# P times V with V as the moving operand in two column tiles, and the result picked and weighted by VectorE, in a one-core decode kernel

## The chip, the cores and the metric

The kernel runs on one core of one Trainium2 chip. The metric is the device time of one execution in microseconds (us). Times quoted are medians of repeated runs. Executions over 1.5% slower than the fastest of the same kernel are left out of the means. A ratio is the mean time of one kernel's runs over the mean of the other's runs of the same rounds, so it is not quite the ratio of the medians quoted; its interval is a 95% one. The span in a profile, from the first to the last instruction, is about 2 us shorter than the time.

## The reference

One decode step, 8 batch rows, sequence length 1: layer norm, attention of 32 query heads on 8 KV heads over the last 2048 of 8192 cached positions, output projection, then a small MLP block. What matters here:

```python
q = (layernorm(x) @ wq)                              # 8 rows, 32 heads of 128
k = k_cache[:, :, Sk - W:, :]                        # W = 2048, 8 KV heads of 128
v = v_cache[:, :, Sk - W:, :]                        # each KV head serves 4 query heads
p = softmax(einsum("bhqd,bhkd->bhqk", q, k) * 128**-0.5)
o = einsum("bhqk,bhkd->bhqd", p, v)
h = x + o.reshape(B, 1, 4096) @ wo
...                                                  # MLP: w3 (512x1792), gelu, w4 (1792x512)
```

K, V and the weights are 79.2 MB, all read once.

## The kernel before

Work is cut into tiles of 2 MB: four KV heads of one batch row, 128 partitions by 64 chunks of 128 columns. Each batch row has two K tiles and two V tiles, each handled in four quarters (`NT`, index `qi`); a quarter is one step of the main loop. Ten buffers hold tiles, and they are filled in the order of use by one queue.

Per step, TensorE transposes 16 chunks of K into PSUM (`pe_T`), ScalarE copies one half out (`act_Elo`), VectorE the other (`dve_Ehi`), and two steps later TensorE multiplies them with q (`pe_QK`). When a batch row's scores are complete, the row maximum (`dve_max`, VectorE) and two exp (`act_exp`, ScalarE) follow, then TensorE transposes P, VectorE masks it (`dve_pT`), and P times V runs.

```python
        def pe_PV(e, v):                      # v = 2 * b + gq: one V tile
            # [...] waits for the tile; the order of (qi, cc), 64 pairs, differs for the last tile
            ot = misc[:, OT].rearrange("d (g a r) -> d g a r", g=GL, r=R)[:, :, gq, :]
            pt = pT_sb[:, :, :].rearrange("p c (g x) -> p c g x", g=GL)
            for n, (qi, cc) in enumerate(seq):
                c = qi * CC + cc
                # [...] waits for the two halves of pT, and of the last V tile
                o = R * (NT * gq + qi)
                ins = e.matmul(ot, slots[:, slot, c * DH:(c + 1) * DH], pt[:, cc, :, o:o + R],
                               start=(n == 0), stop=(n == C - 1), skip_group_check=True)
            ins.then_inc(sem_PV, 1)

        def dve_combine(e, b):                # once per batch row: times 1/L, into oT_all
            e.wait_ge(sem_PV, 2 * (b + 1))
            e.wait_ge(sem_rL, b + 1)
            e.tensor_tensor(oT_all[:, :, b].rearrange("p (q g r) -> p g q r", g=GL, r=R),
                            misc[:, OT].rearrange("p (g q r) -> p g q r", g=GL, r=R),
                            rL[:, :].rearrange("p (g q r) -> p g q r", g=GL, r=R), ALU.mult).then_inc(sem_oT, 1)

        for p in range(NITEM + 2 * NT):       # one step = one quarter of a K tile
            b, t = divmod(p - 2 * NT, 2 * NT) # t = 0..7 within the softmax and PV of batch row b
            if p < NITEM:                     # transposes and evictions of K, one batch row ahead
                # [...] PE: pe_T(k, p); ACT: act_Elo(p); DVE: dve_Ehi(p)
            # [...] PE: pe_QK(p - 2), at t == 0 also pe_QK(p - 1)
            if t == 0:
                DV.append(lambda e, b=b: dve_max(e, b))
            if t in (1, 2):
                AC.append(lambda e, b=b, h=t - 1: act_exp(e, b, h))
            if t == TP:                       # TP = 3
                # [...] PE: transposes of P; DVE: sums of P, dve_pT in two halves; PE, DVE: 1/L
                PE.append(lambda e, b=b: pe_PV(e, 2 * b))
            elif t == 7:
                PE.append(lambda e, b=b: pe_PV(e, 2 * b + 1))
                DV.append(lambda e, b=b: dve_combine(e, b))
```

V is the stationary operand: 64 weight loads of 128x128, and 64 matmuls of 16 columns, per V tile. Each engine works through its list in order, so the place of a piece in the list decides what it can delay (measured: in the changed kernel the row maximum starts at 75.39 us, behind the sums listed ahead of it, though its scores are complete at about 74.3). After the last batch row come the output projection (128 matmuls of 8 columns with Wo stationary) and the MLP.

Of the kernel before, what the change touches and what calls it, by code (L numbers as in the profile page):

```python
# [6 lines left out]
dt = mybir.dt  # L7
# [6 lines left out]
H = 32  # L14
DH = 128
# [22 lines left out]
def bass_sequential_preLN__sliding_block_cached__mixer_s_mlp__decode_kernel(  # L38
# [24 lines left out]
    with es:  # L63
# [28 lines left out]
        pT_sb = sb([128, CC, 128], dt.bfloat16, "pT_sb")  # L92
        maskT = sb([128, 128], dt.bfloat16, "maskT")
        sel = sb([128, H], dt.float32, "sel")
# [4 lines left out]
        lsel = sb([128, H], dt.float32, "lsel")  # L99
        rL = sb([128, H], dt.float32, "rL")  # L100
        iota_f = sb([128, 128], dt.float32, "iota_f")
        ones_f = sb([128, 128], dt.float32, "ones_f")
# [27 lines left out]
        LB = slice(256, 256 + H)  # L130
        misc = ps_t([128, 512], dt.float32, "misc")
        OT = slice(256, 256 + H)
# [27 lines left out]
        sem_PV = S("sem_PV")  # L160
        sem_oT = S("sem_oT")
# [32 lines left out]
        def pool_prog(e):  # L194
# [3 lines left out]
            e.memset(scratch[:], 1.0)  # L198
            e.memset(ones_f[:], 0.25).then_inc(sem_pool, 1)
# [92 lines left out]
        def dve_ident(e):  # L292
# [4 lines left out]
            with nc.allow_low_precision("sums of one 1 and zeros"):  # L297
                ins = e.tensor_reduce(sel[:, 0:GL], ident_f[:, :].rearrange("p (a g) -> p g a", g=GL), AX.X, ALU.add)
            chain(e, ins, "dve_self", dve_self)
            ins = e.tensor_copy(maskT[:, :].rearrange("p (g x) -> p g x", g=GL),  # L300
                                bass.AP(tensor=sel[:, :].tensor, offset=0, ap=[[H, 128], [1, GL], [0, 128 // GL]]))
            chain(e, ins, "dve_self", dve_self)
            e.tensor_reduce(sel[:, :].rearrange("p (a r) -> p a r", r=R),
                            ident_f[:, :].rearrange("p (a q r) -> p a r q", q=NT, r=R),
                            AX.X, ALU.add).then_inc(sem_dveP, 1)
# [170 lines left out]
        def dve_lsel(e, b):  # L476
            e.wait_ge(sem_exp, 2 * (b + 1))
            if b >= 1:
                e.wait_ge(sem_LB, b)
            j = b % 2  # L480
            ins = e.tensor_tensor(lsum[:, :], lcol[:, j, 0:1], lcol[:, j, 1:2], ALU.add)  # L481
            chain(e, ins, "dve_self", dve_self)
            e.tensor_scalar(lsel[:, :], sel[:, :], lsum[:, :], None, ALU.mult).then_inc(sem_lsel, 1)

        def pe_LB(e, b):
            e.wait_ge(sem_lsel, b + 1)
            if b >= 1:
                e.wait_ge(sem_rL, b)
            e.matmul(b6[:, LB], ones_f[:, :], lsel[:, :], start=True, stop=True).then_inc(sem_LB, 1)

        def dve_rL(e, b):
            e.wait_ge(sem_LB, b + 1)
            if b >= 1:
                e.wait_ge(sem_oT, b)
            e.reciprocal(rL[:, :], b6[:, LB]).then_inc(sem_rL, 1)

        def dve_pT(e, b, half):
            e.wait_ge(sem_PT, 2 * b + half + 1)
            if b >= 1:
# [3 lines left out]
            mask_rep = bass.AP(tensor=maskT[:, :].tensor, offset=0, ap=[[128, 128], [0, hc], [1, 128]])  # L503
            e.tensor_tensor(pT_sb[:, half * hc:(half + 1) * hc, :],  # L504
                            kT_ps[n % 2][:, half * W // 2:(half + 1) * W // 2].rearrange("p (c x) -> p c x", x=128),
                            mask_rep, ALU.mult).then_inc(sem_pT, 1)

        def pe_PV(e, v):
# [5 lines left out]
            if gq == 0 and b >= 1:  # L514
                e.wait_ge(sem_oT, b)
            ot = misc[:, OT].rearrange("d (g a r) -> d g a r", g=GL, r=R)[:, :, gq, :]
            pt = pT_sb[:, :, :].rearrange("p c (g x) -> p c g x", g=GL)
            if last:
                seq = [(qi, cc) for qi in range(NT) for cc in range(CC)]
            else:  # L520
                seq = [(qi, cc) for lo in (0, CC // 2) for qi in range(NT) for cc in range(lo, lo + CC // 2)]
            ins = None
            for n, (qi, cc) in enumerate(seq):
                c = qi * CC + cc
                if gq == 0 and n in (0, C // 2):
                    e.wait_ge(sem_pT, 2 * b + 1 + (n > 0))
                if last and c in V_CUT:
                    e.wait_ge(sem_vlast[V_CUT.index(c)], 16)
                o = R * (NT * gq + qi)
# [229 lines left out]
```

## Time and profile before

198.81 us, median of 3 runs (198.02 to 198.83).

| | before |
|---|---|
| bytes read | 79.2 MB, at about 428 GB/s in mid-stream |
| one batch row | 19.3 to 19.6 us of stream (from K tile to K tile, 69.91 to 147.66 us), about 17.8 us of TensorE work |
| last V half landed, last PV done | 178.66 us, 180.1 us |
| output projection | from 180.57 to 186.8 us |

The page's slice rows. The span is cut into 40 equal slices; a digit is the busy share in tenths, PEclk the granted TensorE clock in tenths:

```profile
span 196.6 us, 6327 instructions
...
PEclk9999999999996999999999699969999979755557
DMA  6999999999999999999999999999999999999990
GB/s 215 427 410 430 427 430 427 430 430 430 430 422 427 430 425 430 427 430 430 427 427 433 430 430 427 428 423 423 427 430 433 430 388 382 425 405 338 398 358 21
...
```

The DMA engines are full from the second slice to the last but one: the stream is the limit. The clock is at a half in the tail (0.50 from 178 to 186.5 us).

The groups of instructions by shape, of the kernel before: line, engine, operation, output and inputs, shape, count, then busy us and the mean ns of one, then idle time before them:

```profile
...
L530 PE MATMUL misc<-pT_sb,slots 128*128 128x16 bf16 x1024 | 28.6, 170 | 3.7 <-DVE pT_sb L504 1.9 <-DMA slots<-in_A_v_cache_dram 1.6 <-issue 0.2
L530 PEld LDWEIGHTS misc<-pT_sb,slots 128*128 128x128 bf16 x1024 | 27.3, 97 | 7.7 <-issue 5.9 <-DMA slots<-in_A_v_cache_dram 1.8
...
L693 PE MATMUL b<-slots,gT 128*8 128x256 bf16 x28 | 2.8, 382 | 0.0
...
L537 DVE TENSOR_TENSOR oT_all<-misc,rL 128x32 bf16<-128x32 f32 x8 | 2.4, 300 | 16.0 <-PE misc L530 16.0
...
```

A narrow matmul lasts 170 ns, but 1024 of them take 28.6 us: one starts every 28 ns. The last matmuls of the MLP (L693) run in two column tiles.

The table of two stretches, each one batch row: bounds and length in us, busy us of PE, PEld, DVE, ACT and POOL with counts, then granted clock, DMA share, GB/s:

```profile
...
69.91:89.17 19.26, 17.05 (x313) 12.38 (x310) 9.28 (x20) 10.27 (x12) 0.00 (x0) 1.00 1.01 427
89.17:108.64 19.47, 17.07 (x306) 12.38 (x306) 8.98 (x19) 10.27 (x12) 0.00 (x0) 1.00 1.01 428
...
```

TensorE is busy for 17.06 of some 19.4 us while the DMA share is 1: it has time to spare. The waits of TensorE in total us, times and longest:

```profile
...
PE kT_ps L406 <- DMA slots<-in_A_k_cache_dram: 7.9, 6, 1.7
...
PE S_ps L603 <- issue: 1.9, 1, 1.9
...
```

It waited for K tiles six times (one of them the first). From the first row, 19.26 us less one wait of 1.51 us inside it, TensorE's own need of about 17.8 us per batch row follows. The stream's own pace shows where TensorE waits for it: the K tiles of 89.17 and 147.66 us, three batch rows apart, both ended such a wait, so a batch row of stream takes 19.5 us.

The timeline of TensorE in the tail (start, us, engine, line, operation, count, idle before and what ended it):

```profile
...
158.88 1.15 PE L406 MATMUL kT_ps<-ident_b,slots 128*128 128x128 bf16 x16 [1.25 <-DMA slots<-in_A_k_cache_dram]
...
174.16 1.88 PE L530 MATMUL misc<-pT_sb,slots 128*128 128x16 bf16 x64
...
178.66 0.97 PE L530 MATMUL misc<-pT_sb,slots 128*128 128x16 bf16 x30 [1.41 <-DMA slots<-in_A_v_cache_dram]
...
180.74 3.15 PE L603 MATMUL S_ps<-oT_all,slots 128*128 128x8 bf16 x112
184.12 0.40 PE L603 MATMUL S_ps<-oT_all,slots 128*128 128x8 bf16 x9 [0.23 <-DMA slots<-in_A_wo_dram]
186.46 0.33 PE L603 MATMUL S_ps<-oT_all,slots 128*128 128x8 bf16 x7 [1.93 <-issue]
```

The transposes of the last K tile begin at 158.88 us, as soon as it has landed. PV of the last tile but one takes 1.88 us at a granted clock of 0.50, little more than the 1.75 us it takes at 1.00 (78.12 us). Inside the projection TensorE stands for 1.93 us with nothing to wait for ("issue"), after the 121st matmul.

### The profile page before, as it was taken

How to read it: one execution, taken by the hardware profiler on the slowest of the kernel's cores; microseconds unless marked ns; L12 is line 12 of the kernel's file. 1: busy time of each engine (PE TensorE's matmuls, PEld its weight loads, DVE VectorE, ACT ScalarE, POOL GpSimd, SP SyncE). 2: the span in 40 equal slices, each digit the busy share in tenths (PEclk: the TensorE clock that was granted, in tenths of full speed). 3: DMA queues.
4: the chain of work that ended last, by engine and by line, in shares of the span. 5: the costliest groups of instructions: out<-in, count | busy, mean ns of one | idle time of the engine just before them, and what ended most of it. 6: DMA issues, size and time to landing. Idle time of an engine off the chain costs nothing.

```text
span 196.6 us, 6327 instructions
## 1 busy us (share of the span) xinstructions
PE 159.2 (81%) x2808; PEld 118.4 (60%) x2808; DVE 82.4 (42%) x184; ACT 90.6 (46%) x109; POOL 4.7 (2%) x15
## 2 busy tenths in 40 slices
PE   2027999789999998988897889899979879395555
PEld 0027865566768675755675667677756656185553
DVE  7501445543463457335623473356336514330040
ACT  3300565945392648434753384457535635240040
POOL 8000000000000000000000000000000000000000
PEclk9999999999996999999999699969999979755557
DMA  6999999999999999999999999999999999999990
GB/s 215 427 410 430 427 430 427 430 430 430 430 422 427 430 425 430 427 430 430 427 427 433 430 430 427 428 423 423 427 430 433 430 388 382 425 405 338 398 358 21
DMA packets 10569, 79.57 MB, mean 405 GB/s; under 512 B 672, under 2 KB 4784, under 8 KB 6192
## 3 DMA queue, kind: packets, MB, share of 16 engines
q1 hardware_dynamic: 10544, 79.19, 96.5%
q8 instruction: 22, 0.36, 0.7%
q14 instruction: 3, 0.02, 0.0%
HBM read 79.18 MB, written 0.01 MB: 403 GB/s over the span
## 4 chain that ended last, share of the span: by engine, by line
DMA 56%; PE 28%; SPq 6%; issue 4%; DVE 3%; ACT 3%; ACTq 0%; DVEq 0%
DMA slots<-in_A_k_cache_dram 51%; PE kT_ps L406 16%; PE S_ps L438 6%; SPq L266 5%; DMA slots<-in_A_wo_dram 5%; PE misc L530 3%; ACT P_sb L472 1%; PE b L693 1%; ACT kT_sb L417 1%; PE misc L663 1%; DVE pT_sb L504 1%; PE S_ps L603 0%; PE S_ps L621 0%; DVE mtile L450 0%; SPq L258 0%
## 5 line engine op out<-in xcount | busy, mean ns | idle before, releaser
L417 ACT ACTIVATE kT_sb<-kT_ps 128x1024 bf16<-128x1024 bf16 x64 | 65.5, 1023 | 75.6 <-PE kT_ps L406 75.6
L406 PEld LDWEIGHTS kT_ps<-ident_b,slots 128*128 128x128 bf16 x1024 | 63.7, 104 | 30.0 <-issue 21.5
L406 PE MATMUL kT_ps<-ident_b,slots 128*128 128x128 bf16 x1024 | 73.2, 231 | 7.9 <-DMA slots<-in_A_k_cache_dram 7.9
L423 DVE COPY kT_sb<-kT_ps 128x1024 bf16<-128x1024 bf16 x64 | 43.4, 687 | 61.4 <-PE kT_ps L406 61.4
L438 PE MATMUL S_ps<-kT_sb,qstrip 128*32 128x512 bf16 x256 | 39.0, 614 | 0.0
L530 PEld LDWEIGHTS misc<-pT_sb,slots 128*128 128x128 bf16 x1024 | 27.3, 97 | 7.7 <-issue 5.9
L530 PE MATMUL misc<-pT_sb,slots 128*128 128x16 bf16 x1024 | 28.6, 170 | 3.7 <-DVE pT_sb L504 1.9
L472 ACT ACTIVATE P_sb<-S_ps,mtile 128x1024 bf16<-128x1024 f32 x16 | 17.8, 1113 | 4.8 <-DVE mtile L461 4.4
L406 PE MATMUL kT_ps<-ident_b,P_sb 128*128 128x128 bf16 x128 | 10.6, 231 | 6.6 <-ACT P_sb L472 5.5
L406 PEld LDWEIGHTS kT_ps<-ident_b,P_sb 128*128 128x128 bf16 x128 | 7.8, 103 | 12.0 <-issue 4.4
L504 DVE TENSOR_TENSOR pT_sb<-kT_ps,maskT 128x1024 bf16<-128x1024 bf16 x16 | 10.4, 684 | 0.1
L438 PEld LDWEIGHTS S_ps<-kT_sb,qstrip 128*32 128x32 bf16 x256 | 6.0, 94 | 6.5 <-issue 1.2
L537 DVE TENSOR_TENSOR oT_all<-misc,rL 128x32 bf16<-128x32 f32 x8 | 2.4, 300 | 16.0 <-PE misc L530 16.0
L585 ACT ACTIVATE std<-var,eps_t 128x8 f32<-128x8 f32 x1 | 0.3, 301 | 14.3 <-DVE var L636 14.3
L450 DVE TENSOR_REDUCE mtile<-S_ps 128x1 f32<-128x512 f32 x8 | 5.5, 692 | 3.1 <-PE S_ps L438 3.1
L361 PE MATMUL S_ps<-xlnT,slots 128*128 128x8 bf16 x128 | 3.6, 168 | 3.6 <-DMA slots<-in_A_wq_dram 3.6
L361 PEld LDWEIGHTS S_ps<-xlnT,slots 128*128 128x128 bf16 x128 | 3.5, 104 | 3.6 <-issue 3.6
L603 PE MATMUL S_ps<-oT_all,slots 128*128 128x8 bf16 x128 | 3.9, 168 | 2.2 <-issue 1.9
L341 PE MATMUL b<-ident_b,xln_b 8*128 8x8 bf16 x4 | 0.3, 175 | 6.4 <-DVE xln_b L318 6.4
L603 PEld LDWEIGHTS S_ps<-oT_all,slots 128*128 128x128 bf16 x128 | 3.6, 104 | 2.3 <-issue 2.0
L481 DVE TENSOR_TENSOR lsum<-lcol 128x1 f32<-128x1 f32 x8 | 1.3, 158 | 8.0 <-ACT P_sb L472 8.0
L341 PEld LDWEIGHTS b<-ident_b,xln_b 8*128 8x128 bf16 x4 | 0.2, 116 | 7.3 <-DVE xln_b L318 7.3
(75 smaller groups left out, 59.8 us busy)
## 6 DMA issues: line engine op xcount, KB each, us to landing
slots<-in_A_k_cache_dram SPq DMA_DIRECT2D x16, 2048.0 KB, 41.5
slots<-in_A_v_cache_dram SPq DMA_DIRECT2D x15, 2048.0 KB, 43.3
slots<-in_A_wq_dram SPq DMA_DIRECT2D x1, 4096.0 KB, 12.2
slots<-in_A_wo_dram SPq DMA_DIRECT2D x1, 2048.0 KB, 43.8
slots<-in_A_v_cache_dram SPq DMA_DIRECT2D x2, 1024.0 KB, 13.6
slots<-in_B_w_dram SPq DMA_DIRECT2D x1, 1792.0 KB, 11.6
slots<-in_A_wo_dram SPq DMA_DIRECT2D x1, 1024.0 KB, 16.5
slots<-in_A_wo_dram SPq DMA_DIRECT2D x2, 512.0 KB, 13.0
```

Of the source, the lines that this page charges most:

```text
L266: e.dma_start(dst[:, f0:f0 + (h1 - h0) * D].rearrange("p (h n) -> p h n", n=D), A_wo[h0 * 128:h1 * 128, :].rearrange("(h p) n -> p h n", p ...
L361: ins = e.matmul(S_ps[:, 0, h * B:(h + 1) * B], wq_v[:, kc, h * DH:(h + 1) * DH], xlnT[:, kc * B:(kc + 1) * B], start=(kc == 0), stop=(kc ...
L406: ins = e.matmul(kT_ps[n % 2][:, c * 128:(c + 1) * 128], src[:, c * 128:(c + 1) * 128], ident_b[:, :], is_transpose=True)
L417: e.activation(kT_sb[:, i % NKT, 0:W // 2], kT_ps[step_of[("k", i)] % 2][:, 0:W // 2], ACT.Copy).then_inc(sem_Elo, 1)
L423: e.tensor_copy(kT_sb[:, i % NKT, W // 2:W], kT_ps[step_of[("k", i)] % 2][:, W // 2:W]).then_inc(sem_Ehi, 1)
L438: ins = e.matmul(S_ps[32 * gl:32 * (gl + 1), b % 2, :], qstrip[:, b, GL * gq + gl, o:o + 32], kv[:, gl, :, :], start=(gq == 0 and qi == 0) ...
L450: ins = e.tensor_reduce(mtile[:, 2, 0:1], S_ps[:, j, :], AX.X, ALU.max)
L472: e.activation(P_sb[:, half * W // 2:(half + 1) * W // 2].rearrange("r (k g) -> r k g", g=GL), s_rep, ACT.Exp, bias=mtile[:, j, 0:1], scal ...
L504: e.tensor_tensor(pT_sb[:, half * hc:(half + 1) * hc, :], kT_ps[n % 2][:, half * W // 2:(half + 1) * W // 2].rearrange("p (c x) -> p c x", ...
L530: ins = e.matmul(ot, slots[:, slot, c * DH:(c + 1) * DH], pt[:, cc, :, o:o + R], start=(n == 0), stop=(n == C - 1), skip_group_check=True)
L537: e.tensor_tensor(oT_all[:, :, b].rearrange("p (q g r) -> p g q r", g=GL, r=R), misc[:, OT].rearrange("p (g q r) -> p g q r", g=GL, r=R), ...
L603: ins = e.matmul(hT_ps[:, k * B:(k + 1) * B], wo_at(h)[:, k * 128:(k + 1) * 128], oT_all[:, h, :], start=False, stop=(h == H - 1), skip_gr ...
```

## The change

The intent: exchange the operands of P times V. P (64 columns: four heads by four quarters by four rows) becomes stationary, and V moves, 512 columns at a time, in two column tiles of the array, so that a V tile needs 16 matmuls in place of 64. The result is a matrix of 64 rows by four quarters, of which only the blocks with matching quarter are wanted. VectorE picks and normalises them: four dependent operations multiply each quarter's block with a mask that holds 1/L and add them up; one fp32 matmul per V tile then sums the two column tiles and transposes, and VectorE copies the result.

The diff, cut to its core (constants, the set-up of the selection masks, the new layout of the P mask, one more small operation in the 1/L step and some waits are left out):

```diff
@@ pe_PV @@
-            for n, (qi, cc) in enumerate(seq):
-                [...]
-                ins = e.matmul(ot, slots[:, slot, c * DH:(c + 1) * DH], pt[:, cc, :, o:o + R],
-                               start=(n == 0), stop=(n == C - 1), skip_group_check=True)
+            if v >= 1:
+                e.wait_ge(sem_O1, v)
+            vq = slots[:, slot, :].rearrange("p (q c d) -> p c q d", q=NT, d=DH)
+            groups = [(0, 2), (2, 4)] if last else [(0, NT)]
+            for n, (q0, q1) in enumerate(groups):
+                if last:
+                    e.wait_ge(sem_vlast[n], 16)
+                for cc in range(CC):
+                    [...]
+                    a = cc % 2
+                    ins = e.matmul(misc[64 * a:64 * (a + 1), q0 * DH:q1 * DH].rearrange("p (q d) -> p q d", d=DH),
+                                   pT_sb[:, gq, cc, :], vq[:, cc, q0:q1, :],
+                                   start=(n == 0 and cc < 2), stop=(n == len(groups) - 1 and cc >= CC - 2),
+                                   tile_position=(0, 64 * a), skip_group_check=True)
             ins.then_inc(sem_PV, 1)

-        def dve_combine(e, b): [...]
+        def dve_O1(e, v):
+            [...]
+            ins = e.tensor_scalar(o_sum[:, :], misc[:, 0:DH], mrl[:, gq, 0:1], None, ALU.mult)
+            for q in range(1, NT):
+                chain(e, ins, "dve_self", dve_self)
+                ins = e.scalar_tensor_tensor(o_sum[:, :], misc[:, q * DH:(q + 1) * DH], mrl[:, gq, q:q + 1],
+                                             o_sum[:, :], ALU.mult, ALU.add)
+            ins.then_inc(sem_O1, 1)
+
+        def pe_oT(e, v):
+            e.wait_ge(sem_O1, v + 1)
+            [...]
+            e.matmul(b6[:, OT], o_sum[:, :], hsel[:, :], start=True, stop=True).then_inc(sem_oTm, 1)
+
+        def dve_oT(e, v):
+            [...]
+            e.tensor_copy(oT_all[:, GL * R * gq:GL * R * (gq + 1), b], b6[:, OT]).then_inc(sem_oT, 1)
@@ main loop, behind the transposes and evictions of a step @@
+            for v, (at_o1, at_mm, at_cp) in late.items():
+                if p == at_o1:
+                    DV.append(lambda e, v=v: dve_O1(e, v))
+                if p == at_mm:
+                    PE.append(lambda e, v=v: pe_oT(e, v))
+                if p == at_cp:
+                    DV.append(lambda e, v=v: dve_oT(e, v))
@@ t == TP @@
                 PE.append(lambda e, b=b: pe_PV(e, 2 * b))
+                late[2 * b] = (p + 1, p + 2, p + 3)
             elif t == 7:
                 PE.append(lambda e, b=b: pe_PV(e, 2 * b + 1))
-                DV.append(lambda e, b=b: dve_combine(e, b))
+                late[2 * b + 1] = (p + 1, p + 2, p + 3)
@@ behind the loop @@
+        DV.append(lambda e: dve_O1(e, NTILE - 1))
+        PE.append(lambda e: pe_oT(e, NTILE - 1))
+        DV.append(lambda e: dve_oT(e, NTILE - 1))
```

So the sums of a V tile come one step after its PV, the summing matmul two steps after, the copy three.

More of the change, by code (lines that the diff above doesn't have):

```diff
@@ L91, in bass_sequential_preLN__sliding_block_cached__mixer_s_mlp__decode_kernel @@
         P_sb = sb([128, CC * 128], dt.bfloat16, "P_sb")
-        pT_sb = sb([128, CC, 128], dt.bfloat16, "pT_sb")
-        maskT = sb([128, 128], dt.bfloat16, "maskT")
-        sel = sb([128, H], dt.float32, "sel")
+        pT_sb = sb([128, 2, CC, 64], dt.bfloat16, "pT_sb")
+        maskT = sb([128, CC // 2 * GL, 32], dt.bfloat16, "maskT")
+        sel = sb([128, GL], dt.float32, "sel")
+        headc = sb([128, NT * R], dt.float32, "headc")
+        lspread = sb([128, 128], dt.float32, "lspread")
+        par_sel = sb([128, 2, GL * R], dt.float32, "par_sel")
+        hsel = sb([128, GL * R], dt.float32, "hsel")
+        gq_of = sb([128, 2], dt.float32, "gq_of")
+        qi_of = sb([128, NT], dt.float32, "qi_of")
+        mrl = sb([128, 2, NT], dt.float32, "mrl")
+        o_sum = sb([128, DH], dt.float32, "o_sum")
         mtile = sb([128, 3, 32], dt.float32, "mtile")
@@ L98, in bass_sequential_preLN__sliding_block_cached__mixer_s_mlp__decode_kernel @@
         lsum = sb([128, 1], dt.float32, "lsum")
-        lsel = sb([128, H], dt.float32, "lsel")
-        rL = sb([128, H], dt.float32, "rL")
+        lsel = sb([128, 2], dt.float32, "lsel")
+        rL = sb([128, 2], dt.float32, "rL")
         iota_f = sb([128, 128], dt.float32, "iota_f")
-        ones_f = sb([128, 128], dt.float32, "ones_f")
         oT_all = sb([128, H, B], dt.bfloat16, "oT_all")
@@ L129, in bass_sequential_preLN__sliding_block_cached__mixer_s_mlp__decode_kernel @@
         xT_ps = b6[:, 0:256].bitcast(dt.bfloat16)
-        LB = slice(256, 256 + H)
+        LB = slice(256, 258)
+        OT = slice(320, 320 + GL * R)
         misc = ps_t([128, 512], dt.float32, "misc")
-        OT = slice(256, 256 + H)
         H3 = slice(384, 384 + FC * B)
@@ L160, in bass_sequential_preLN__sliding_block_cached__mixer_s_mlp__decode_kernel @@
         sem_PV = S("sem_PV")
+        sem_O1 = S("sem_O1")
+        sem_oTm = S("sem_oTm")
         sem_oT = S("sem_oT")
@@ L197, in pool_prog @@
             e.memset(zrow_b[:], 0.0)
-            e.memset(scratch[:], 1.0)
-            e.memset(ones_f[:], 0.25).then_inc(sem_pool, 1)
+            e.memset(scratch[:], 1.0).then_inc(sem_pool, 1)
             e.iota(iota_f[:], [[1, 128]], base=0, channel_multiplier=-1,
@@ L299, in dve_ident @@
             chain(e, ins, "dve_self", dve_self)
-            ins = e.tensor_copy(maskT[:, :].rearrange("p (g x) -> p g x", g=GL),
-                                bass.AP(tensor=sel[:, :].tensor, offset=0, ap=[[H, 128], [1, GL], [0, 128 // GL]]))
+            ins = e.tensor_copy(maskT[:, :, :].rearrange("p (c g) x -> p c g x", g=GL),
+                                bass.AP(tensor=sel[:, :].tensor, offset=0, ap=[[GL, 128], [0, CC // 2], [1, GL], [0, 32]]))
             chain(e, ins, "dve_self", dve_self)
-            e.tensor_reduce(sel[:, :].rearrange("p (a r) -> p a r", r=R),
-                            ident_f[:, :].rearrange("p (a q r) -> p a r q", q=NT, r=R),
-                            AX.X, ALU.add).then_inc(sem_dveP, 1)
+            with nc.allow_low_precision("sums of one 1 and zeros"):
+                e.tensor_reduce(headc[:, :].rearrange("p (g r) -> p g r", r=R),
+                                ident_f[:, :].rearrange("p (g x r) -> p g r x", g=GL, r=R), AX.X, ALU.add)
+                e.tensor_reduce(par_sel[:, :, :].rearrange("p a (g r) -> p a g r", r=R),
+                                ident_f[:, :].rearrange("p (a g q r) -> p a g r q", a=2, g=GL, r=R), AX.X, ALU.add)
+                e.tensor_reduce(gq_of[:, :], ident_f[:, :].rearrange("p (g a x) -> p a g x", g=GL, a=2), AX.XY, ALU.add)
+                ins = e.tensor_reduce(qi_of[:, :], ident_f[:, :].rearrange("p (a q r) -> p q a r", q=NT, r=R), AX.XY, ALU.add)
+            chain(e, ins, "dve_self", dve_self)
+            hc = bass.AP(tensor=headc[:, :].tensor, offset=0, ap=[[NT * R, 128], [R, GL], [0, NT], [1, R]])
+            for a in range(2):
+                e.tensor_scalar(lspread[:, 64 * a:64 * (a + 1)].rearrange("p (g q r) -> p g q r", g=GL, r=R),
+                                hc, 0.25, None, ALU.mult)
+            e.tensor_tensor(hsel[:, :], par_sel[:, 0, :], par_sel[:, 1, :], ALU.add).then_inc(sem_dveP, 1)
         DV.append(dve_ident)
@@ L482, in dve_lsel @@
             chain(e, ins, "dve_self", dve_self)
-            e.tensor_scalar(lsel[:, :], sel[:, :], lsum[:, :], None, ALU.mult).then_inc(sem_lsel, 1)
+            e.tensor_scalar(lsel[:, :], gq_of[:, :], lsum[:, :], None, ALU.mult).then_inc(sem_lsel, 1)
         def pe_LB(e, b):
@@ L487, in pe_LB @@
             if b >= 1:
+                e.wait_ge(sem_oT, 2 * b)
                 e.wait_ge(sem_rL, b)
-            e.matmul(b6[:, LB], ones_f[:, :], lsel[:, :], start=True, stop=True).then_inc(sem_LB, 1)
+            e.matmul(b6[:, LB], lspread[:, :], lsel[:, :], start=True, stop=True).then_inc(sem_LB, 1)
         def dve_rL(e, b):
             e.wait_ge(sem_LB, b + 1)
-            if b >= 1:
-                e.wait_ge(sem_oT, b)
-            e.reciprocal(rL[:, :], b6[:, LB]).then_inc(sem_rL, 1)
+            ins = e.reciprocal(rL[:, :], b6[:, LB])
+            chain(e, ins, "dve_self", dve_self)
+            e.tensor_tensor(mrl[:, :, :],
+                            bass.AP(tensor=rL[:, :].tensor, offset=0, ap=[[2, 128], [1, 2], [0, NT]]),
+                            bass.AP(tensor=qi_of[:, :].tensor, offset=0, ap=[[NT, 128], [0, 2], [1, NT]]),
+                            ALU.mult).then_inc(sem_rL, 1)
         def dve_pT(e, b, half):
@@ L502, in dve_pT @@
             hc = CC // 2
-            mask_rep = bass.AP(tensor=maskT[:, :].tensor, offset=0, ap=[[128, 128], [0, hc], [1, 128]])
-            e.tensor_tensor(pT_sb[:, half * hc:(half + 1) * hc, :],
-                            kT_ps[n % 2][:, half * W // 2:(half + 1) * W // 2].rearrange("p (c x) -> p c x", x=128),
-                            mask_rep, ALU.mult).then_inc(sem_pT, 1)
+            e.tensor_tensor(pT_sb[:, :, half * hc:(half + 1) * hc, :].rearrange("p a c (g x) -> p (c g) a x", g=GL),
+                            kT_ps[n % 2][:, half * W // 2:(half + 1) * W // 2].rearrange("p (m a x) -> p m a x", a=2, x=16),
+                            maskT[:, :, :].rearrange("p m (a x) -> p m a x", a=2), ALU.mult).then_inc(sem_pT, 1)
         def pe_PV(e, v):
@@ L513, in pe_PV @@
                 e.wait_ge(sem_slot[slot], 16 * use)
-            if gq == 0 and b >= 1:
-                e.wait_ge(sem_oT, b)
-            ot = misc[:, OT].rearrange("d (g a r) -> d g a r", g=GL, r=R)[:, :, gq, :]
-            pt = pT_sb[:, :, :].rearrange("p c (g x) -> p c g x", g=GL)
-            if last:
-                seq = [(qi, cc) for qi in range(NT) for cc in range(CC)]
-            else:
-                seq = [(qi, cc) for lo in (0, CC // 2) for qi in range(NT) for cc in range(lo, lo + CC // 2)]
@@ L522, in pe_PV @@
-            ins = None
-            for n, (qi, cc) in enumerate(seq):
-                c = qi * CC + cc
-                if gq == 0 and n in (0, C // 2):
-                    e.wait_ge(sem_pT, 2 * b + 1 + (n > 0))
-                if last and c in V_CUT:
-                    e.wait_ge(sem_vlast[V_CUT.index(c)], 16)
-                o = R * (NT * gq + qi)
-                ins = e.matmul(ot, slots[:, slot, c * DH:(c + 1) * DH], pt[:, cc, :, o:o + R],
-                               start=(n == 0), stop=(n == C - 1), skip_group_check=True)
@@ L532, in pe_PV @@
-            ins.then_inc(sem_PV, 1)
-        def dve_combine(e, b):
-            e.wait_ge(sem_PV, 2 * (b + 1))
-            e.wait_ge(sem_rL, b + 1)
-            e.tensor_tensor(oT_all[:, :, b].rearrange("p (q g r) -> p g q r", g=GL, r=R),
-                            misc[:, OT].rearrange("p (g q r) -> p g q r", g=GL, r=R),
-                            rL[:, :].rearrange("p (g q r) -> p g q r", g=GL, r=R), ALU.mult).then_inc(sem_oT, 1)
+            if v >= 1:
+                e.wait_ge(sem_O1, v)
@@ new lines, in pe_PV @@
+            vq = slots[:, slot, :].rearrange("p (q c d) -> p c q d", q=NT, d=DH)
+            groups = [(0, 2), (2, 4)] if last else [(0, NT)]
+            ins = None
+            for n, (q0, q1) in enumerate(groups):
+                if last:
+                    e.wait_ge(sem_vlast[n], 16)
+                for cc in range(CC):
+                    if gq == 0 and cc in (0, CC // 2):
+                        e.wait_ge(sem_pT, 2 * b + 1 + (cc > 0))
+                    a = cc % 2
[3 more added lines that the diff above has]
+                                   tile_position=(0, 64 * a), skip_group_check=True)
@@ new lines, in pe_PV @@
+            ins.then_inc(sem_PV, 1)
+        def dve_O1(e, v):
+            b, gq = divmod(v, 2)
+            e.wait_ge(sem_PV, v + 1)
+            if gq == 0:
+                e.wait_ge(sem_rL, b + 1)
+            if v >= 1:
+                e.wait_ge(sem_oTm, v)
+            ins = e.tensor_scalar(o_sum[:, :], misc[:, 0:DH], mrl[:, gq, 0:1], None, ALU.mult)
+            for q in range(1, NT):
+                chain(e, ins, "dve_self", dve_self)
+                ins = e.scalar_tensor_tensor(o_sum[:, :], misc[:, q * DH:(q + 1) * DH], mrl[:, gq, q:q + 1],
+                                             o_sum[:, :], ALU.mult, ALU.add)
+            ins.then_inc(sem_O1, 1)
@@ L541, in bass_sequential_preLN__sliding_block_cached__mixer_s_mlp__decode_kernel @@
+        def pe_oT(e, v):
+            e.wait_ge(sem_O1, v + 1)
+            e.wait_ge(sem_rL, v // 2 + 1)
+            if v >= 1:
+                e.wait_ge(sem_oT, v)
+            e.matmul(b6[:, OT], o_sum[:, :], hsel[:, :], start=True, stop=True).then_inc(sem_oTm, 1)
+        def dve_oT(e, v):
+            b, gq = divmod(v, 2)
+            e.wait_ge(sem_oTm, v + 1)
+            e.tensor_copy(oT_all[:, GL * R * gq:GL * R * (gq + 1), b], b6[:, OT]).then_inc(sem_oT, 1)
+        late = {}
         for p in range(NITEM + 2 * NT):
@@ L593, in pe_proj @@
             e.wait_ge(sem_exp, 2 * NB)
-            e.wait_ge(sem_oT, NB)
+            e.wait_ge(sem_oT, 2 * NB)
             for k in range(KC):
```

## The prediction

> **What bounds it now.** The input stream. The slice rows show the DMA engines at 90% or more from the second slice to the last but one, at about 428 GB/s; 79.2 MB at that rate is 185 us. In the table of stretches one pair of batch halves (two K and two V tiles) takes 19.3 to 19.9 us, DMA share 1.00. TensorE needs about 17.8 us of it: the waits view has it idle for K tiles five times, 1.1 to 1.7 us each, in mid-stream. V is reissued far ahead (issue to landing 41 to 43 us), so a late slot release starves nothing. After the last V half lands (178.66 in the timeline) a serial tail follows: last PV to 180.1, combine, 128 output-projection matmuls (third Wo piece at 184.1, then 1.93 us of "issue" idle), 186.8, then the MLP, 9.8 us.
>
> **What changes.** PV: 64 matmuls of 16 columns per V tile, 1.75 us (about 27 ns each), become 16 of 512 columns in two column tiles. Transposes stream 128 columns in 62 ns (16 in 1.00 us), so 512 should cost about 0.22 to 0.25 us, an estimate. That two column tiles run together the MLP's last matmuls show: 28 of 256 columns in 2.64 us, while one of them lasts 382 ns. So 8 pairs cost 1.8 to 2.0 us: no gain, although busy instructions fall by 750. [...]
>
> Added per V tile: on VectorE four dependent 128x128 operations from PSUM, about 0.3 us each (the 128x32 one takes 0.30, the 128x512 reduction 0.69), so 1.25 us, and a 0.3 us copy instead of half a 0.30 us combine; on TensorE an fp32 128x16 matmul, 0.3 us (the 128x32 one is 0.3 to 0.4). The mask multiply should stay at 0.68 us, and the extra 1/L step is small.
>
> **What is on the path.** Mid-stream almost nothing directly. But the second V tile's four operations come ahead of the row maximum in VectorE's order, and the end of the scores matmuls and of those PV matmuls lie only about 2 us apart: I expect maximum, exp and P transposes to move about 1 us per batch. With the summing matmuls TensorE's need rises from 17.8 to some 19.2 to 20.3 us, about the stream's 19.6. So it stops catching up: the backlog of about 2 us that it has at batch 0 (first K waits only at 89 us) stays, or grows by some us.
>
> In the tail two new chains (1.25 weighted sum + 0.4 matmul + 0.35 copy) stand in series, the first before the last PV, and PV's 512-column streams feel the half clock of the last slices (0.5), which 16-column matmuls did not. The Wo wait and the 1.93 us stall hide part. Sum: +1 to +4 us; a grown backlog could add more.
>
> **Time.** 201.0 us; 8 in 10 between 197.8 and 206. Faster by over 2%: 0.04; within: 0.70; slower: 0.26.
>
> **Right or wrong, in the profile.** PV per tile at 1.8 to 2.0 us mid-stream; VectorE busy from 82 to about 105 us; DMA still full to about 190 us; fewer K waits by TensorE, and later; row maximum about 1 us later after the scores; projection starting at 182 to 186 instead of 180.6; matmuls from 2808 to about 2090.
>
> **What would make it wrong.** Column tiles that run serially, or weight loads that show (PV near 3.5 us): TensorE then bounds every batch, 208 us or more. Full backlog recovery, or the instruction stall vanishing with the shorter program: 198 us. A mask multiply slowed by its 16-element runs delays every batch.

One sentence, on weight loads, is cut from the recorded text at the mark: no trace of this case shows what it said. The sum of +1 to +4 us held no term for it and stands as it was.

## The result, and the profile after

205.37 us (median of 4 runs, 203.53 to 205.77) against 198.74 us (4 runs): ratio 1.0321, interval 1.0276 to 1.0366. The change is 3.2% slower.

The page's slice rows of the changed kernel:

```profile
span 203.4 us, 4997 instructions
...
PEclk9999999999999999999999999999999999859757
DMA  6999999999999999999999999999999999999300
GB/s 208 419 435 432 425 438 419 432 428 420 435 432 422 441 420 435 422 428 438 419 435 424 435 428 425 432 432 428 419 441 422 386 432 408 395 390 411 134 0 5
...
```

The stream's last full slice is the 37th, and the last two slices and more, some 13 us, move next to nothing; before the change that stretch was one slice of 5 us. The stream no longer sets the end. The granted clock is no worse than before (0.958 in the mean against 0.905).

The groups of the changed kernel that are new:

```profile
...
L547 PE MATMUL misc<-slots,pT_sb 128*64 128x512 bf16 x240 | 30.5, 398 | 2.1 <-DVE pT_sb L525 2.1
...
L563 DVE SCALAR_TENSOR_TENSOR o_sum<-misc,mrl,o_sum 128x128 f32<-128x128 f32 x48 | 16.8, 351 | 1.7
L547 PEld LDWEIGHTS misc<-slots,pT_sb 128*64 128x64 bf16 x272 | 15.7, 113 | 14.7 <-issue 7.1
...
L572 PE MATMUL b<-hsel,o_sum 128*128 128x16 f32 x32 | 6.3, 273 | 9.5 <-DVE o_sum L563 9.5
...
```

A wide matmul lasts 398 ns, but two run at once: in the PV of 81.47 us the two of a pair start 4 to 31 ns apart, and the 8 pairs take 1.86 us, 0.23 us each, at a granted clock of 1.00. The table of two stretches, each one batch row from TensorE's point of view:

```profile
...
83.33:103.50 20.17, 18.21 (x217) 11.49 (x216) 11.35 (x29) 10.27 (x12) 0.00 (x0) 1.00 1.00 428
143.80:163.92 20.12, 18.17 (x216) 11.44 (x215) 11.35 (x29) 10.28 (x12) 0.00 (x0) 1.00 1.01 416
...
```

A batch row takes 20.15 us, the same every time (P's transposes start at 59.14, 79.28, 99.43, 119.58, 139.73 and 159.88 us). That is 0.65 us more than the 19.5 us that the stream needed before. The waits of TensorE:

```profile
...
PE b L572 <- DVE o_sum L563: 9.5, 16, 1.6
...
PE kT_ps L424 <- DVE kT_sb L441: 2.2, 6, 0.4
...
PE kT_ps L424 <- DMA slots<-in_A_k_cache_dram: 1.2, 1, 1.2
...
```

In place of six waits for K tiles there is one (the first of all), and there are 16 for the weighted sums. Where these lie shows the timeline of TensorE within one batch row:

```profile
...
75.53 0.40 PE L572 MATMUL b<-hsel,o_sum 128*128 128x16 f32 x2 [0.20 <-DVE o_sum L563]
...
77.75 1.05 PE L424 MATMUL kT_ps<-ident_b,slots 128*128 128x128 bf16 x16 [0.37 <-DVE kT_sb L441]
...
81.47 1.92 PE L547 MATMUL misc<-slots,pT_sb 128*64 128x512 bf16 x16 [0.30 <-DVE pT_sb L525]
...
84.87 1.07 PE L424 MATMUL kT_ps<-ident_b,slots 128*128 128x128 bf16 x16
86.60 0.40 PE L572 MATMUL b<-hsel,o_sum 128*128 128x16 f32 x2 [0.66 <-DVE o_sum L563]
...
```

The summing matmul of the first V tile (start 86.60) stands in TensorE's list right behind the transposes of 84.87, but VectorE's sums, which begin only behind an eviction of K, are not done: 0.66 us idle. For the second V tile (75.53) the wait is 0.20 us. The transposes at 77.75 wait another 0.37 us for an eviction of K by VectorE. VectorE's timeline shows why that one is late:

```profile
...
73.37 0.69 DVE L441 COPY kT_sb<-kT_ps 128x1024 bf16<-128x1024 bf16 x1 [2.70 <-PE kT_ps L424]
73.98 0.34 DVE L560 TENSOR_SCALAR o_sum<-misc,mrl 128x128 f32<-128x128 f32 x1
74.36 1.12 DVE L563 SCALAR_TENSOR_TENSOR o_sum<-misc,mrl,o_sum 128x128 f32<-128x128 f32 x3
75.39 0.68 DVE L468 TENSOR_REDUCE mtile<-S_ps 128x1 f32<-128x512 f32 x1
...
```

The four operations of the sums (73.98 to 75.48) come ahead of the row maximum (75.39), which could have started when the scores were complete, at about 74.3. So the maximum, the evictions behind it and exp are about 1 us late.

The tail of the changed kernel:

```profile
...
163.92 1.07 PE L424 MATMUL kT_ps<-ident_b,slots 128*128 128x128 bf16 x16
...
179.86 3.62 PE L547 MATMUL misc<-slots,pT_sb 128*64 128x512 bf16 x16
185.09 0.40 PE L572 MATMUL b<-hsel,o_sum 128*128 128x16 f32 x2 [1.61 <-DVE o_sum L563]
185.41 1.94 PE L547 MATMUL misc<-slots,pT_sb 128*64 128x256 bf16 x32
...
189.93 3.53 PE L654 MATMUL S_ps<-oT_all,slots 128*128 128x8 bf16 x128
...
```

The transposes of the last K tile begin at 163.92 us, against 158.88 us before: TensorE comes out of mid-stream 5.04 us late; this is the lag of the texts below. PV of the last tile but one takes 3.62 us at a granted clock of 0.50, against 1.92 us at 1.00 in mid-stream. The projection starts at 189.8 us, 9.2 us later than before, but its 128 matmuls run without a stop, and it ends at 193.5 us, 6.7 us later than before.

### The profile page after: what moved, and what is told of

It reads as the page before. It is cut to its first block, busy times and chain, and to the rows that moved or that the text cites. A ratio compares the mean times of both kernels' runs of the same rounds, so it can differ in the third digit from the quotient of the medians.

```text
span 203.4 us, 4997 instructions
## 1 busy us (share of the span) xinstructions
PE 164.8 (81%) x2088; PEld 107.8 (53%) x2088; DVE 103.2 (51%) x270; ACT 90.9 (45%) x109; POOL 4.6 (2%) x14
## 4 chain that ended last, share of the span: by engine, by line
PE 50%; DVE 20%; issue 13%; DMA 8%; ACT 7%; SPq 0%; ACTq 0%; DVEq 0%
PE kT_ps L424 20%; PE misc L547 16%; DMA slots<-in_A_k_cache_dram 8%; PE S_ps L456 8%; DVE o_sum L563 8%; ACT P_sb L490 5%; DVE o_sum L560 3%; DVE mtile L468 2%; DVE pT_sb L525 2%; PE b L572 2%; PE S_ps L654 2%; ACT kT_sb L435 1%; PE b L744 1%; PE misc L714 1%; DVE mrow L470 1%
## 5 line engine op out<-in xcount | busy, mean ns | idle before, releaser
L424 PEld LDWEIGHTS kT_ps<-ident_b,slots 128*128 128x128 bf16 x1024 | 60.3, 101 | 30.5 <-issue 29.2
L424 PE MATMUL kT_ps<-ident_b,slots 128*128 128x128 bf16 x1024 | 70.0, 224 | 3.4 <-DVE kT_sb L441 2.2
L456 PE MATMUL S_ps<-kT_sb,qstrip 128*32 128x512 bf16 x256 | 38.3, 613 | 0.0
L547 PE MATMUL misc<-slots,pT_sb 128*64 128x512 bf16 (+1 forms) x272 | 32.4, 383 | 2.1 <-DVE pT_sb L525 2.1
L547 PEld LDWEIGHTS misc<-slots,pT_sb 128*64 128x64 bf16 x272 | 15.7, 113 | 14.7 <-issue 7.1
L490 ACT ACTIVATE P_sb<-S_ps,mtile 128x1024 bf16<-128x1024 f32 x16 | 17.8, 1115 | 11.6 <-DVE mtile L479 11.5
L563 DVE SCALAR_TENSOR_TENSOR o_sum<-misc,mrl,o_sum 128x128 f32<-128x128 f32 x48 | 16.8, 351 | 1.7
L572 PE MATMUL b<-hsel,o_sum 128*128 128x16 f32 x32 | 6.3, 273 | 9.5 <-DVE o_sum L563 9.5
L572 PEld LDWEIGHTS b<-hsel,o_sum 128*128 128x128 f32 x32 | 4.8, 188 | 13.9 <-DVE o_sum L563 13.9
L560 DVE TENSOR_SCALAR o_sum<-misc,mrl 128x128 f32<-128x128 f32 x16 | 5.5, 344 | 6.3 <-PE misc L547 6.3
```

The lines of the kernel that those rows point to most:

```text
L424: ins = e.matmul(kT_ps[n % 2][:, c * 128:(c + 1) * 128], src[:, c * 128:(c + 1) * 128], ident_b[:, :], is_transpose=True)
L456: ins = e.matmul(S_ps[32 * gl:32 * (gl + 1), b % 2, :], qstrip[:, b, GL * gq + gl, o:o + 32], kv[:, gl, :, :], start=(gq == 0 and qi == 0) ...
L490: e.activation(P_sb[:, half * W // 2:(half + 1) * W // 2].rearrange("r (k g) -> r k g", g=GL), s_rep, ACT.Exp, bias=mtile[:, j, 0:1], scal ...
L547: ins = e.matmul(misc[64 * a:64 * (a + 1), q0 * DH:q1 * DH].rearrange("p (q d) -> p q d", d=DH), pT_sb[:, gq, cc, :], vq[:, cc, q0:q1, :], ...
L560: ins = e.tensor_scalar(o_sum[:, :], misc[:, 0:DH], mrl[:, gq, 0:1], None, ALU.mult)
L563: ins = e.scalar_tensor_tensor(o_sum[:, :], misc[:, q * DH:(q + 1) * DH], mrl[:, gq, q:q + 1], o_sum[:, :], ALU.mult, ALU.add)
```

## The experiments

My theory after this: nothing in the new form is too slow in itself. TensorE waits for the sums in its list, and the maximum waits behind the sums in VectorE's list. That lifts a batch row from about 17.8 to 20.15 us, just over what the stream needs, and only the excess is paid, gathered row by row (six rows lie between the transposes of 43.03 us and the last K tile at 163.92 us). The rivals: the added VectorE work and the wide PV cost the time wherever they stand; or the loss is made in the tail.

### First: the summing matmul of the first V tile one step later

```diff
-                late[2 * b] = (p + 1, p + 2, p + 3)
+                late[2 * b] = (p + 1, p + 3, p + 4)
```

> Only the summing matmul of the first V tile of each batch, and its copy, move one step later in program order; all work is kept. In the changed kernel TensorE stands 0.65 us before that matmul in every batch, waiting for VectorE's weighted sums. Order theory (the loss in mid-stream is TensorE waiting in program order for the sums, twice per batch, which made a batch 20.15 us against some 19.6 us of stream): that wait goes to about 0, a batch takes about 19.5 us, the lag of about 5 us at the last K tile shrinks to about 0.5 to 1.5 us, time about 201 (200 to 202). Rival (the added VectorE work and the new PV form as such cost the time, wherever they stand): a batch stays at about 20.1 us and the time at about 205.

Measured: 200.28 us (198.49 to 200.45), ratio to before 1.0063 (1.0016 to 1.011). P's transposes start every 19.28 us. The waits of TensorE:

```profile
...
PE b L572 <- DVE o_sum L563: 4.9, 9, 1.6
...
PE kT_ps L424 <- DMA slots<-in_A_k_cache_dram: 1.2, 1, 1.2
...
```

The waits for the sums fall from 16 to 9 and from 9.5 to 4.9 us: seven waits of 0.65 us are gone, one per batch row. 0.87 us less per batch row brought back 5 us of 6.6. The same work is done, so the rival of work as such falls. The profile is of the fastest of the four runs (198.49 us), and in it the lag is gone (the last K tile begins at 158.25 us); where the other three, 200.23 to 200.45 us, lose about 1.8 us no trace shows.

### Second: the sums of the second V tile behind the row maximum

```diff
+                if kind == "p" and i >= 1 and c == CT // 2:    # between the halves of P's transposes
+                    pe_oT(e, 2 * i - 1)
 [...]
+                if b >= 1:                                      # ahead of the sums of P
+                    DV.append(lambda e, b=b: dve_oT(e, 2 * b - 1))
 [...]
-                late[2 * b + 1] = (p + 1, p + 2, p + 3)
+                late[2 * b + 1] = (p + 3, None, None)
```

> Only the weighted sums of the second V tile of each batch move: behind the row maximum of the next batch instead of ahead of it, their summing matmul between the two halves of the P transposes, where TensorE waits for exp anyway. All work is kept. Order theory: row maximum, exp and P transposes come about 1 us earlier, the stalls before the transposes that follow go, a batch needs about 18.9 us of TensorE, so the stream bounds again (19.6 us) and the lag at the last K tile goes to about 0 to 1 us; time about 200.5 (199.5 to 202). Rival (work as such): unchanged, about 205.

Measured: 198.18 us (198.07 to 198.25), ratio to before 0.9977 (0.9957 to 0.9997). P's transposes start every 19.15 us (57.45 to 134.05), 1.0 us less, and the last K tile begins at 157.46 us. The wait of 0.65 us of the first V tiles is still there:

```profile
...
PE b L574 <- DVE o_sum L565: 7.8, 9, 1.6
...
```

I expected 200.5 us, with a tail that costs 2 us; the whole loss was gone instead. That was a hint that the wide tail costs less than I thought.

### Third: both moves

The two diffs above together.

> Both moves together, all work kept. Order theory: TensorE needs about 18.2 us per batch, waits for K tiles again as before the change (several waits), the mid-stream loss is gone, and what is left against the kernel before is the tail alone: PV in wide streams at the half clock (3.6 against 1.9 us for the last tile but one) and two chains of weighted sums, summing matmul and copy. Time 200 to 201.5, hardly better than the better of the two single moves. Rival (work as such): about 205.

Measured: 198.13 us (197.72 to 199.77), ratio to before 0.9991 (0.9944 to 1.0037), better than the 200 to 201.5 us that I expected with the wide tail. While TensorE had no K tile to wait for, P's transposes were 18.29 us apart (56.62 to 74.91). Then it waits for K tiles again, as the kernel before did:

```profile
...
PE kT_ps L426 <- DMA slots<-in_A_k_cache_dram: 6.4, 5, 2.4
...
```

Here the batch row has 1.9 us less than in the changed kernel, twice the saving of a single move, and the time is no better than with the second move alone (198.13 against 198.18 us). Below the stream's pace nothing more was won.

### Fourth: the old PV in the last batch row only

The changed kernel, mid-stream untouched; PV and normalisation of the last batch row as before the change:

```diff
+            if b == NB - 1:
+                [...] for n, (qi, cc) in enumerate(seq):      # as before: V stationary, 16 columns
+                    pt = pT_sb[:, gq, cc, :].rearrange("p (g x) -> p g x", g=GL)[:, :, R * qi:R * (qi + 1)]
+                    ins = e.matmul(ot, slots[:, slot, c * DH:(c + 1) * DH], pt, [...])
 [...]
-        DV.append(lambda e: dve_O1(e, NTILE - 1))
-        PE.append(lambda e: pe_oT(e, NTILE - 1))
-        DV.append(lambda e: dve_oT(e, NTILE - 1))
+        DV.append(lambda e: dve_combine(e, NB - 1))           # with 1/L of this batch row in the old form
```

> The changed kernel with PV and normalisation of the last batch alone done as before the change (V stationary, 16 moving columns, one combine); mid-stream is left as changed, with its lag of about 5 us. Order theory: the lag at the last K tile stays at about 5 us, the tail from the last K tile to the projection loses two chains of about 2 us and 1.7 us of slow PV, and V and Wo have long landed: time about 201.5 (200.5 to 202.5). Rival that the tail causes the whole loss: about 199.

Measured: 204.55 us (204.32 to 204.92), ratio to before 1.03 (1.0272 to 1.0328). So the tail does not make the loss. But I had expected 3 to 4 us from it, and got less than one. The page's line of the DMA queue that fetches instructions (packets, MB, share), and the timeline of TensorE:

```profile
...
q8 instruction: 17, 0.28, 0.5%
...
186.74 0.41 PE L567 MATMUL misc<-pT_sb,slots 128*128 128x16 bf16 x9 [2.47 <-issue]
...
187.81 3.20 PE L696 MATMUL S_ps<-oT_all,slots 128*128 128x8 bf16 x114
191.85 0.51 PE L696 MATMUL S_ps<-oT_all,slots 128*128 128x8 bf16 x14 [0.84 <-issue]
...
```

In the narrow PV and in the projection, TensorE stands for 2.47 and 0.84 us with nothing to wait for. Another part of the shortfall is not the tail's: in this execution the first PV took 3.17 us, against 1.92 in the changed kernel (I read this as a stretch at the low clock; the mean granted clock was 0.941 against 0.958). P's transposes followed at 60.41 us, against 59.14, and its last K tile begins at 165.16 us, 1.24 us later than in the changed kernel. From there to the end of the span it takes 37.3 us against 39.5, so the old tail itself won 2.1 us in these two executions.

From the first stop to the second it issued 9, 4 and 114 matmuls, 127 in all (128 if one record is missing). In the kernel before, the same count lies between the stops ahead of the last two matmuls of PV (0.23 us) and the one of 1.93 us: 2, 4 and 121. With a weight load each, that is 254 to 256 instructions. I read these stops as TensorE outrunning its instruction supply. The trace of the kernel before holds the fetches: 22 packets of 16 KB on the queue q8, for 2808 matmuls and as many weight loads, so about 255 a packet if they carry these alone (an estimate). One packet landed at 178.32 us, and the stop of 0.23 us ended at 179.86; the next was on its way from 184.23 to 185.17 us, TensorE stopped at 184.52, and went on at 186.46. So both stops ended after such a packet had landed, by 1.54 and 1.29 us, which fits the reading. Why the second packet comes so late, setting out only 0.29 us before TensorE stopped, is open. The wide form, with 32 matmuls in 1.9 us (185.41 us in the changed kernel), has no such stop.

### Fifth: both moves and the old tail

> Both order moves, and the last batch's PV and normalisation as before the change. My prediction's tail term says that the wide tail costs 1 to 4 us over the old one where there is no lag: this then beats the two moves alone by that much, 195 to 197. Rival, formed after the old tail alone won only 0.8 us: the old tail's 64 narrow matmuls per V tile and the 128 of the projection outrun TensorE's instruction supply (idle put down to issue, after every 128 matmuls or so), which the wide form does not, and that gives its shorter chain back: 198 to 199, with 2 to 3 us of issue idle in the tail.

Measured: 197.24 us (197.05 to 197.92), ratio to before 0.9917 (0.9886 to 0.9949): the best version, 0.8% under the kernel before. The time lies between the two forecasts, 0.2 us above the first and 0.8 us under the rival. Against the two moves alone (0.9991, another chip job, both set against the kernel before) the old tail wins 0.7%, some 1.5 us; but the two intervals touch (0.9944 and 0.9949), the medians differ by 0.9 us and the spans of the two profiled executions by 0.3 us. So what the wide tail costs without the lag is not shown closer than 0.3 to 1.5 us. The tail's lines:

```profile
...
177.40 1.02 PE L569 MATMUL misc<-pT_sb,slots 128*128 128x16 bf16 x32 [1.59 <-DMA slots<-in_A_v_cache_dram]
...
184.70 0.51 PE L700 MATMUL S_ps<-oT_all,slots 128*128 128x8 bf16 x14 [1.87 <-issue]
...
```

The stop is there too (1.87 us). The last V half arrived at 177.40 us, 1.26 us ahead of the kernel before, and that is about the gain over it. Why the stream was ahead there is open: at the K tile of about 147.3 us the two differ by 0.4 us. The lead does not come from the old tail: the DMA instructions for the last V halves begin at 161.95 to 162.36 us in all seven runs with V moving (161.97 here, 161.96 with the two moves alone), and at 163.36 to 163.58 us in the five with V stationary throughout.

### Sixth: only a warm clock

The changed kernel with 40 extra matmuls of 128 columns, thrown away, while TensorE waits for the last exp:

```diff
+        def pe_warm(e):
+            e.wait_ge(sem_exp, 2 * (NB - 1))
+            for k in range(40):
+                e.matmul(S_ps[:, NB % 2, 0:128], ident_b[:, :], ident_b[:, :], start=True, stop=True)
 [...]
+                if b == NB - 1:                     # ahead of the transposes of P
+                    PE.append(lambda e: pe_warm(e))
```

> The changed kernel with 40 extra 128-column matmuls on TensorE (their result is thrown away) where it waits for the last exp, so that the clock does not drop; order and lag unchanged. If the half clock is a term of the loss: PV of the last tile but one goes from 3.6 to about 1.9 us, time 205.4 to about 203.5 (203 to 204.3). If the clock is not granted or the tail is bound elsewhere: 205 to 205.6.

Measured: 203.16 us (202.54 to 205.33), ratio to before 1.0231 (1.0157 to 1.0305).

```profile
...
179.52 1.92 PE L547 MATMUL misc<-slots,pT_sb 128*64 128x512 bf16 x16 [0.30 <-DVE pT_sb L525]
```

PV of the last tile but one takes 1.92 us in place of 3.62. From the last K tile (163.73 us) to the end of the span it takes 37.8 us, against 39.5 in the changed kernel. So the half clock was a term of the loss, 1.7 us of it in these traces, where the lag makes the tail TensorE's. The times alone say less: one of the four runs took 205.33 us, and the interval overlaps that of the changed kernel. That the clock falls because TensorE stands idle is my reading; what was measured is this: in the changed kernel TensorE waited 2.48 us for the exp, and behind it, from 177.56 to 179.86 us, the granted clock was 0.50; with the 40 matmuls in that wait (2.39 us), PV ran at its mid-stream pace, and the run's mean granted clock was 0.972 against 0.958. Narrow matmuls, at 28 ns each, hardly felt the half clock (1.88 against 1.75 us), while the wide ones took 3.62 us in place of 1.92.

### Seventh and eighth: instructions shifted in the kernel before

118 (or 60) narrow matmuls in the opening, thrown away, where TensorE waits for the query weights:

```diff
+        def pe_pad(e):
+            e.wait_ge(sem_dveP, DVEP_XLN)
+            for k in range(118):                   # eighth: 60
+                e.matmul(misc[:, 0:8], ident_b[:, :], ident_b[:, 0:8], start=True, stop=True)
+        PE.append(pe_pad)
```

> The kernel before with 118 narrow matmuls (result thrown away) in the opening, where TensorE waits for the query weights: nothing else changes, but every later instruction stands 236 instructions further on. If the 1.93 us idle inside the projection is instruction supply, in blocks of 128 matmul pairs, the boundary that lay 7 matmuls before the projection's end falls just behind it: no issue idle there, time 1 to 1.9 us less, about 197 to 197.7. If it is the landing of Wo or anything fixed in time: the idle stays at the 121st matmul and the time at 198.7.

> The same with 60 matmuls. Instruction supply: the idle moves some 60 matmuls ahead within the projection, to about its 61st, of 1.5 to 3 us; time 198 to 199. Fixed in time or tied to Wo: it stays at the 121st.

Measured: 198.51 us with 118 (ratio 0.9976, 0.9945 to 1.0006) and 198.65 us with 60 (ratio 0.9984, 0.9956 to 1.0012), neither told from before. The timeline with 118:

```profile
...
180.33 0.24 PE L609 MATMUL S_ps<-oT_all,slots 128*128 128x8 bf16 x3
180.80 3.76 PE L609 MATMUL S_ps<-oT_all,slots 128*128 128x8 bf16 x125 [0.23 <-issue]
...
188.36 1.65 PE L669 MATMUL misc<-uT,slots 128*128 128x8 bf16 x56 [2.60 <-DMA slots<-in_B_w_dram]
...
```

The stop of 1.93 us is gone from the 121st matmul, though Wo lands as before; 0.23 us stand behind the third matmul, 118 places earlier. So this stop hung on the place in the instruction stream, not on data. (The padding makes one of its own, 1.60 us in the query projection.) But no time is won: the MLP's weights are now what TensorE waits for (2.60 us): in the kernel before the stop was hidden by the stream. With 60, I expected the stop at about the 61st matmul; there was no stop in the projection at all. The expectation missed; why the stop was absent is not shown.

### Ninth and tenth: a dose of TensorE time in the kernel before

The kernel before, with 24 (or 40) matmuls of 128 columns behind the first PV of each batch row but the last:

```diff
+        def pe_dose(e):
+            for k in range(24):                    # tenth: 40
+                e.matmul(misc[:, 0:128], ident_b[:, :], ident_b[:, :], start=True, stop=True)
 [...]
                 PE.append(lambda e, b=b: pe_PV(e, 2 * b))
+                if b < NB - 1:
+                    PE.append(lambda e: pe_dose(e))
```

> The kernel before, untouched but for 24 matmuls of 128 columns (result thrown away) behind the first PV of each batch but the last: at 60 ns each, as the extra matmuls of the warm run took, 1.4 us more of TensorE per batch, so about 19.2 us, still under the stream's 19.6. Threshold theory (only what a batch needs beyond the stream is paid): time within 1 us of before, about 199, with fewer or no waits for K tiles. Rival (added TensorE time is paid in full once a batch): 7 x 1.4 = 10 us more, about 208; a share of it if half hidden.

> The same with 40: 2.4 us more, about 20.2 us per batch, which is what the changed kernel's batch takes, but with PV, sums, copies and tail as before the change. Threshold theory: 7 batches each exceed the stream by some 0.6 us and the waits for K tiles before the change (about 1.5 us per batch, plus a backlog of 2 us) no longer help: a lag of 4 to 6 us at the last K tile, no waits for K tiles, time 202.5 to 205. If the changed kernel's loss were in the wide PV or in its tail, this stays under 200.

| | batch row, mean of five | waits for K tiles | time | ratio to before |
|---|---|---|---|---|
| 24 matmuls | 19.2 us | 2, in all 1.5 us | 199.49 us (198.62 to 201.74) | 1.0032 (0.9982 to 1.0083) |
| 40 matmuls | 20.3 us | 1 (the first of all) | 207.11 us (206.25 to 210.4) | 1.0405 (1.0369 to 1.0441) |

(Batch rows from the starts of P's transposes: 58.73 to 154.96, and 59.41 to 161.01.)

1.4 us per batch row cost nothing that is told from noise; 1 us more cost 7.6 us. That is this kernel's threshold, made in the kernel before, with the old PV, no sums and the old tail. With 24, the last K tile begins at 161.03 us: a lag of 2.15 us, which the tail hid. The second overshot my 202.5 to 205: three of its seven doses took 3.97, 3.80 and 3.88 us in place of 2.39 (I read this as a lower clock; the mean of 20.3 us holds one of them, and an issue stop of 0.55 us; an undisturbed batch row took 19.84 us), the last K tile begins at 168.55 us, a lag of 9.67 us where I had expected 4 to 6, and the tail has two issue stops (2.81 and 0.68 us), none of which I had put in.

## Why the prediction was right or wrong

- **The bound before (the stream, 428 GB/s, TensorE with time to spare): right.** The doses show it. (The 19.9 us came from a stretch, 139 to 158.88 us, that does not begin at a row's edge, and the shortest of the five waits was 0.8 us.)
- **PV at 1.8 to 2.0 us, "no gain": right.** 16 wide matmuls: 1.86 us from start to the next start (81.47 to 83.33). The 64-column weight loads (113 ns each) did not show beside the streams: in these 1.86 us the loads were busy for 0.99 us, and a pair of matmuls took 0.23 us. The last risk that the prediction names did not show either: the mask multiply takes 684 ns in both kernels.
- **VectorE's work: right.** Busy 103.2 us against 105 forecast; one of the four operations lasts 0.35 us against 0.3.
- **The maximum about 1 us later: right.** The second experiment took it away, together with the place of the second summing matmul, and won 1.0 us per batch row.
- **TensorE's need of 19.2 to 20.3 us per batch row: right by its upper end,** 20.15 us. But its make-up lacked a term. The prediction added matmuls and the late maximum; it did not see that the summing matmul of the first V tile is issued one step before the sums can be done, 0.65 us per batch row. The first experiment removed that.
- **The step that failed is the size of the backlog: "Sum: +1 to +4 us; a grown backlog could add more", with a backlog that "stays, or grows by some us".** The sum left mid-stream almost out and gave the tail nearly all. Measured, the lag at the last K tile was 5.04 us. Of the 6.8 us between the two spans, 5.04 are there at the last K tile, 1.6 are added up to the end of the projection and 0.1 in the MLP. With a need just under the stream's pace, as in the first and second experiments (19.28 and 19.15 us), there is no lag (last K tile at 158.25 and 157.46 us, against 158.88 before) in the profiled executions; just over it, as in the changed kernel (20.15 us), the excess adds up row by row. A forecast of 19.2 to 20.3 us around a stream of 19.6 holds both cases, and I gave the middle one number when it had two outcomes.
- **The tail: right in size, but not where most of the loss lay.** Two chains and the half clock (0.50) were both there: 0.3 to 1.5 us without the lag (fifth experiment against the third), 1.7 us of clock with it (sixth). "The Wo wait and the 1.93 us stall hide part" held too: the projection started 9.2 us late and ended 6.7 us late: the stall and the Wo wait were gone. I did not foresee that the narrow tail has such stops of its own, which is part of why the old tail alone won so little (fourth).
- **"Projection starting at 182 to 186": wrong,** 189.8 us, for the same backlog. With both moves it starts at 182.3 us. The stream was full to about 188 us, close to the 190 forecast.

What stays open: why the stream is ahead of the kernel before by about 1 us or more at the last V halves in the versions with V moving, why the instruction packets come late in the narrow form, and what three of the four runs of the first experiment lose.

## What to carry to other kernels

In this kernel, whose stream is the limit, added engine time cost nothing up to the stream's pace, and beyond it the excess added up round by round, less a little that the tail hid (a lag of 2.15 us cost nothing that is told from noise, one of 9.67 us lengthened the span by 7.9 us). So compare each engine's need per round with the stream's time per round, and when the range of your estimate has the stream's time inside it (here 19.2 to 20.3 us around 19.5), predict two outcomes and not a mean. Here the new chain between TensorE and VectorE cost by its places in their lists more than by its length (ratio 1.0321 before the two moves, 0.9991 after them): find for each wait the earliest moment at which its input can exist, and put it behind that. Moving two pieces, with the same work, turned 3.2% slower into no loss.
